# Cosine attention and a dense block on one core: norm steps moved between visits, dense work shifted by one visit, one exponential held back

## The chip, the cores and the metric

The kernel runs on one core of a Trainium2 chip. The core has a matrix engine (TensorE, PE in the profile; its weight loads are PEld), a vector engine (VectorE, DVE), an engine for functions of one element (ScalarE, ACT), a general engine (GpSimd, POOL) and a queue engine (SyncE, SP). They run side by side, each through its own queue in order, and wait for each other through semaphores. The metric is the time of one execution on the device in microseconds (us), as a median over runs.

## The reference

Inputs are q, k and v of shape (8 batches, 12 heads, 448 tokens, 64), a number tau = 0.1, and two weight matrices.

```python
q_n = q / (norm(q, axis=-1) + 1e-6)
k_n = k / (norm(k, axis=-1) + 1e-6)
scores = q_n @ k_n.transpose(0, 1, 3, 2) / tau
attn = exp(scores - max(scores));  attn = attn / (sum(attn) + 1e-9)
x = (attn @ v).transpose(0, 2, 1, 3).reshape(3584, 768)
h = x @ w_in                      # 768 -> 2048
out = maximum(0.01 * h, h) @ w_out    # 2048 -> 768
```

So each batch is attention over normalized queries and keys, and the 3584 rows of all batches then pass a dense block of two layers with a leaky activation.

## The kernel before

**Attention.** The 448 tokens of a batch are taken as 4 blocks of 112 (NT, PK). Heads are handled in 6 pairs (p from 0 to 5), and pairs in 3 groups (g) of four heads. For a pair, `scores` works in two halves. A half is two key blocks: for each one, two matmuls (one head each) write a PSUM tile `sc`, and one exponential on ScalarE (L209) turns it into `pe`. There are two `sc` buffers. When both pairs of a group are done, `sums` multiplies `pe` with ones and `values` multiplies it with v, 16 matmuls each (L216), into the two `pv` buffers. `inverse` takes the reciprocal of the sums on VectorE (L239) and frees its buffer, and `x_write` multiplies and writes x, transposed (L253 and L254 in even batches, L256 in odd ones). `weigh` strings these together, once for each half (s) of the group's values.

**Norms.** They are made one batch ahead. `norm_squares` (L123) squares on VectorE or GpSimd (in the opening on ScalarE too, L121), `norm_reduce` sums 64 elements on VectorE (L126), `norm_root` takes the root as Ln and Exp on ScalarE (L138, L139), `norm_inverse` adds and inverts on VectorE (L143, L144), `norm_apply` scales, mostly on GpSimd in pieces of two heads (L151). `norm_sums` is squares and reduction together. The scaled q and k must then be turned so that the 64 elements lie on partitions: batches 0 to 3 by TensorE (`turn_pair`, L179, with copies on VectorE, L189), later ones by a DMA transpose (`turn`, L168).

**Dense block.** Rows are cut into chunks of 3 or 4 tiles of 128, in turn: chunk c needs x of batch c. `layer1` makes one of 16 groups of 6 matmuls (L274), 384 or 512 columns wide, and the activation on ScalarE (L279); `layer2` makes a group of 16 matmuls (L287), a copy on ScalarE (L293) and the output write on SyncE's queue. Both take their PSUM from two `mm` buffers, which `turn_pair` uses too.

**The order.** It is written out by hand and nothing reorders it. An opening does batch 0. Then a loop runs over batches 1 to 7 and in each over 12 visits (n, a pair and a half). One visit does: the scores of that half; one `weigh` if one is owed (visits 4 and 5, 8 and 9, and 0 and 1 of the next batch); the steps of `after_scores`, where norm steps and loads are set by batch and visit; dense groups, by `fill`; the turns of `after_dense`. `fill` takes groups from a list with a cost each (layer 1 about 1.0 or 1.3, layer 2 2.65) until the running cost reaches a goal. The goal rises evenly with the visits, so that chunk c is worked through from visit 2 of batch c + 1 to visit 1 of batch c + 2; the first chunk has 14 visits.

```python
if b == 1 or (b == 2 and n < 2):
    fill(chunk_end[0] * (12 * (b - 1) + n + 1) / 14)
else:
    c = b - 1 if n >= 2 else b - 2
    start = chunk_end[c - 1]
    fill(start + (chunk_end[c] - start) * ((n - 2) % 12 + 1) / 12)
```

From batch 3 on, the steps for the next batch stand at visits 0 to 7: sums of q at 0, root at 1, sums of k at 2 with the scaling of q, root of k at 3, scaling of k at 4, transposes at 5 and 7. After the loop come the last two `weigh` and what is left of the list.

Of the kernel before, what the change touches and what calls it, by code (L numbers as in the profile page):

```python
# [9 lines left out]
BF16 = mybir.dt.bfloat16  # L10
ACTF = mybir.ActivationFunctionType
# [5 lines left out]
def kernel(  # L17
# [17 lines left out]
    nc = tc.nc  # L35
# [3 lines left out]
    NT = 4  # L39
# [59 lines left out]
    def load_w_out(n):  # L99
        nc.gpsimd.dma_start(  # L100
            out=w_out_sb[:, :, n * NH : (n + 1) * NH], in_=w_out_r[:, :, n * NH : (n + 1) * NH]
        )
# [67 lines left out]
            in_=xn.rearrange("p g t h d -> p (g t h d)"),  # L170
        )

    def turn_pair(b, p):
        g, j = divmod(p, 2)
        tp = pmm.tile([128, 2, NT, PK], BF16, name="mm")
        for i, what in enumerate("qk"):
            xn = st[what + "n", b]
            for t in range(NT):
                nc.tensor.matmul(  # L179
                    out=tp[:, i, t, :],  # L180
                    lhsT=xn[:, g, t, 2 * j : 2 * j + 2, :].rearrange("p h d -> p (h d)"),
                    rhs=ident, is_transpose=True,
                    start=(i == 0 and t == 0), stop=(i == 1 and t == NT - 1),
                )
        for i, what in enumerate("qk"):
            xt = turned(b, what)[:, : NT * HP * PK].rearrange(
                "d (g t j n) -> d g t j n", g=G, t=NT, j=2
            )
            nc.vector.tensor_copy(out=xt[:, g, :, j, :], in_=tp[:, i])  # L189


    def scores(b, p, half):
        qT, kT = st["qT", b], st["kT", b]
        g, j = divmod(p, 2)
        q5 = qT[:, : NT * HP * PK].rearrange("d (g t j n) -> d g t j n", g=G, t=NT, j=2)
        if half == 0:
            st["pe", b, p] = epool.tile([PK, NT, 2, S], BF16, name="pe")
        pe = st["pe", b, p]
        wide = 128 if b > 3 else PK
        for ki in (2 * half, 2 * half + 1):  # L200
            sc = psc.tile([128, 2, 512], F32, name="sc")
            o = ((g * NT + ki) * 2 + j) * PK
            for a in range(2):
                r = slice(64 * a, 64 * a + 64)
                nc.tensor.matmul(  # L205
                    out=sc[:wide, a, :S], lhsT=kT[r, o : o + wide], rhs=q5[r, g, :, j, :],
                    start=True, stop=True,
                )
            nc.scalar.activation(  # L209
                out=pe[:, ki], in_=sc[:PK, :, :S], func=ACTF.Exp, scale=inv_tau  # L210
            )

    def columns(dst, b, g, weights):
        for ki in range(NT):
# [17 lines left out]
    def sums(b, g):  # L232
        sm = ppv.tile([128, S], F32, name="pv")
        columns(sm, b, g, lambda a, ki: ones[:PK, :])
        return sm

    def inverse(b, g, sm):
        st["rs", b, g] = wk.tile([128, S], F32, name="rs")
        nc.vector.reciprocal(st["rs", b, g], sm)  # L239
        if g == 0:  # L240
            x_place(b)

    def values(b, g, s, po=None):
        vb = st["v", b]
        if po is None:
            po = ppv.tile([128, S], F32, name="pv")
        columns(po, b, g, lambda a, ki: vb[:, G * a + g, ki, 32 * s : 32 * s + 32])
        return po

    def x_write(b, g, s, po):  # L250
        rs, x, kt = st["rs", b, g], st["x", b], 2 * g + s
        if b % 2 == 0:
            nc.vector.tensor_mul(x[:, kt, 0:384], po[:, 0:384], rs[:, 0:384])  # L253
            nc.vector.tensor_mul(st["x64", b][:, kt, :], po[:, 384:S], rs[:, 384:S])  # L254
        else:
            nc.vector.tensor_mul(x[:, kt, 64:512], po, rs)  # L256
# [121 lines left out]
    norm_apply(0, "q", V, 2, 3)  # L378
    scores(0, 2, 0)
    sm = sums(0, 0)  # L380
    po = values(0, 0, 0)
    inverse(0, 0, sm)
    scores(0, 2, 1)
    load_w_out(0)
    x_write(0, 0, 0, po)
    scores(0, 3, 0)
    x_write(0, 0, 1, values(0, 0, 1))
    scores(0, 3, 1)
    turn_pair(0, 4)
    turn_pair(0, 5)  # L390
    norm_squares(1, "q", P, 0, 1)
    norm_squares(1, "k", P, 0, 1)
    load(1, "v")
    scores(0, 4, 0)
    sm = sums(0, 1)
    po = values(0, 1, 0)
    inverse(0, 1, sm)
    x_write(0, 1, 0, po)
    scores(0, 4, 1)
    load_w_out(1)  # L400
    norm_reduce(1, "q", 0, 1)
    norm_reduce(1, "k", 0, 1)
    scores(0, 5, 0)
    x_write(0, 1, 1, values(0, 1, 1))
    norm_root(1, "q", 0, 1)
    norm_root(1, "k", 0, 1)
    scores(0, 5, 1)
    norm_inverse(1, "q", 0, 1)
    norm_inverse(1, "k", 0, 1)
    norm_apply(1, "q", P, 0, 1)  # L410
# [18 lines left out]
    def after_scores(b, n):  # L429
        if b + 2 < B and b > 1 and n < 2:  # L430
            load(b + 2, "qk"[n])
        if b + 1 == B:
            return
        if b > 1 and n == 2:
            load(b + 1, "v")
        if b == 1:
            if n == 0:
                load(2, "q")
                norm_sums(1, "q", 1, 2)
                norm_sums(1, "k", 1, 2)  # L440
            elif n == 1:
                load(2, "k")
                norm_root(1, "q", 1, 2)
                norm_root(1, "k", 1, 2)
                norm_sums(1, "q", 2, 3)
                norm_sums(1, "k", 2, 3)
            elif n == 2:
                load(2, "v")
                for what in "qk":
                    norm_inverse(1, what, 1, 2)  # L450
                    norm_apply(1, what, P, 1, 2)
                norm_root(1, "q", 2, 3)
                norm_root(1, "k", 2, 3)
            elif n == 3:
                for what in "qk":
                    norm_inverse(1, what, 2, 3)
                    norm_apply(1, what, P, 2, 3)
            elif n == 5:
                load(3, "q")
            elif n == 6:  # L460
                norm_sums(2, "q")
                load(3, "k")
            elif n == 7:
                norm_root(2, "q")
                norm_sums(2, "k")
            elif n == 8:
                norm_root(2, "k")
                norm_inverse(2, "q")
                norm_inverse(2, "k")
                for g in range(G):  # L470
                    norm_apply(2, "q", P, g, g + 1)
                    norm_apply(2, "k", V if g == 0 else P, g, g + 1)
        elif b == 2:
            if n == 3:
                norm_sums(3, "q")
            elif n == 5:
                norm_root(3, "q")
                norm_sums(3, "k")
            elif n == 6:
                norm_root(3, "k")  # L480
                norm_inverse(3, "q")
                norm_inverse(3, "k")
                for g in range(G):
                    norm_apply(3, "q", P, g, g + 1)
                    norm_apply(3, "k", P, g, g + 1)
        elif n == 0:
            norm_sums(b + 1, "q")
        elif n == 1:
            norm_root(b + 1, "q")
        elif n == 2:  # L490
            norm_sums(b + 1, "k")
            norm_inverse(b + 1, "q")
            norm_apply(b + 1, "q", P)
        elif n == 3:
            norm_root(b + 1, "k")
        elif n == 4:
            norm_inverse(b + 1, "k")
            norm_apply(b + 1, "k", P)
        elif n == 5:
            turn(b + 1, "q")  # L500
        elif n == 7:
            turn(b + 1, "k")

    turns = {
        (1, 3): (1, 2), (1, 4): (1, 3), (1, 5): (1, 4, 5), (1, 10): (2, 0, 1),
        (1, 11): (2, 2, 3), (2, 1): (2, 4, 5), (2, 9): (3, 0, 1), (2, 10): (3, 2, 3),
        (2, 11): (3, 4, 5),
    }

    def after_dense(b, n):  # L510
# [3 lines left out]

    owed = []
    for b in range(1, B):
        for p in range(HP):
            for half in range(2):  # L520
                n = 2 * p + half
                scores(b, p, half)
                if owed:
                    weigh(*owed.pop(0))
                if half == 1 and p % 2 == 1:
                    owed += [(b, p // 2, 0), (b, p // 2, 1)]
                after_scores(b, n)
                if b == 1 or (b == 2 and n < 2):
                    fill(chunk_end[0] * (12 * (b - 1) + n + 1) / 14)
                else:  # L530
                    c = b - 1 if n >= 2 else b - 2
                    start = chunk_end[c - 1]
                    fill(start + (chunk_end[c] - start) * ((n - 2) % 12 + 1) / 12)
                after_dense(b, n)
    fill(spent[0] + 1.0)
    weigh(*owed[0])
    fill(chunk_end[B - 2] - 3.0)
    weigh(*owed[1])
    fill(1e9)

# [34 lines left out]
```

## Time and profile before

| | |
|---|---|
| time, median of 3 runs | 486.72 us (484.1 to 489.21) |
| span of the profiled run | 485.3 us |
| mean granted clock of TensorE | 0.982 of full |
| VectorE, reciprocals of row sums | 24 of 2.96 us |
| VectorE, squares and reduction of a whole q or k | 1.9 and 3.35 us |
| ScalarE, exponentials | 192 of 0.92 us, 0.86 back to back |
| ScalarE, activations of layer 1 | 128 of 0.5 or 0.6 us |
| GpSimd, scaling | 86 pieces of 1.06 us |
| DMA transposes, issue to landing | 5.1 us (q) and 7.3 us (k) in the median, 11.0 at most |

A line of the timeline gives start, length, engine, line of the kernel, what is written from what, shapes and count; in brackets is how long the engine stood idle before it and what it waited for. Matmuls overlap, so the length of a group of them is from its first start to its last end. "PEclk" is the clock that TensorE was granted, as a share of full speed or in tenths.

### The profile page before, as it was taken

What the parts mean: (1) busy time and instruction counts of PE and PEld (TensorE: products, weight loads), DVE (VectorE), ACT (ScalarE), POOL (GpSimd) and SP (SyncE); (2) the same over time, 40 slices, a digit from 0 to 9 for tenths busy, and PEclk for the clock granted to TensorE, in tenths of its full rate; (3) what the DMA queues carried; (4) which work ended last, traced back from release to release, by engine and by line L of the source; (5) the groups of instructions that cost most, each with busy time, mean ns of one, the idle gap of its engine ahead of it and who ended that gap; (6) DMA issues with size and microseconds to landing.
All of it is one profiled execution on the core that took longest, in us unless ns stands there. A gap on an engine that the chain in (4) does not pass through costs nothing.

```text
span 485.3 us, 8021 instructions
## 1 busy us (share of the span) xinstructions
PE 438.5 (90%) x3380; PEld 213.6 (44%) x3392; DVE 217.4 (45%) x265; ACT 265.9 (55%) x429; POOL 127.3 (26%) x152
## 2 busy tenths in 40 slices
PE   0786988899899989998999989997999999989996
PEld 0332454454355544442345434442445444444463
DVE  5967959657632871347412672338403312321000
ACT  3874856546654377455564577454664567433411
POOL 7457160740280047002720036002620000000000
PEclk9999899999999999998999999997999999998999
DMA  9999995194019335924393244215331200120022
GB/s 124 212 197 203 202 148 80 50 135 69 1 29 167 55 53 93 170 64 57 58 148 90 54 70 86 63 49 74 57 58 50 63 20 1 34 65 1 0 66 65
DMA packets 68482, 39.82 MB, mean 82 GB/s; under 512 B 24160, under 2 KB 67680, under 8 KB 68448
## 3 DMA queue, kind: packets, MB, share of 16 engines
q0 software_dynamic: 37728, 22.81, 33.6%
q1 hardware_dynamic: 30720, 16.52, 14.3%
q8 instruction: 26, 0.43, 0.4%
q14 instruction: 8, 0.07, 0.0%
HBM read 45.61 MB, written 11.01 MB: 117 GB/s over the span
## 4 chain that ended last, share of the span: by engine, by line
PE 70%; DVE 14%; ACT 8%; issue 5%; POOL 1%; DMA 1%; DVEq 0%; ACTq 0%; POOLq 0%
PE mm L274 26%; PE mm L287 25%; PE pv L216 10%; PE sc L205 7%; DVE rs L239 5%; ACT pe L209 4%; DVE q_n L123 2%; DVE q_ni L126 2%; ACT hT L279 2%; DVE k_ni L126 2%; PE mm L179 2%; POOL q_n L151 1%; DVE k_n L123 1%; DMA qk_bf<-in_q_dram 1%; ACT osb L293 1%
## 5 line engine op out<-in xcount | busy, mean ns | idle before, releaser
L274 PE MATMUL mm<-xT,w_in_sb 128*128 128x384 bf16 (+1 forms) x756 | 161.9, 362 | 16.2 <-ACT hT L279 5.3
L209 ACT ACTIVATE pe<-sc 112x896 bf16<-112x896 f32 x192 | 165.0, 917 | 15.0 <-PE sc L205 14.9
L287 PE MATMUL mm<-w_out_sb,hT 128*128 128x384 bf16 x896 | 153.3, 326 | 0.1
L239 DVE RECIPROCAL rs<-pv 128x448 f32<-128x448 f32 x24 | 71.0, 2957 | 165.4 <-PE pv L216 165.4
L274 PEld LDWEIGHTS <-w_in_sb 128*128 128x128 bf16 x768 | 72.8, 99 | 102.1 <-issue 45.0
L287 PEld LDWEIGHTS <-hT 128*128 128x128 bf16 x896 | 84.6, 98 | 67.8 <-issue 14.5
L279 ACT ACTIVATE hT<-mm 128x384 bf16<-128x384 f32 (+1 forms) x128 | 68.7, 545 | 68.0 <-PE mm L274 67.3
L293 ACT COPY osb<-mm 128x384 f32<-128x384 f32 x56 | 26.7, 478 | 106.8 <-PE mm L287 81.5
L151 POOL TENSOR_TENSOR q_n<-qk_bf,q_ni 112x512 bf16<-112x512 bf16 x42 | 43.5, 1063 | 92.1 <-DVE q_ni L144 37.0
L205 PE MATMUL sc<-qT,kT 64*112 64x448 bf16 (+1 forms) x384 | 59.6, 379 | 8.8 <-ACT pe L209 5.4
L151 POOL TENSOR_TENSOR k_n<-qk_bf,k_ni 112x512 bf16<-112x512 bf16 x44 | 45.4, 1059 | 16.8 <-DVE k_ni L144 12.4
L216 PE MATMUL pv<-pe,v_bf 112*32 112x448 bf16 x736 | 44.1, 360 | 3.6 <-DVE rs L239 3.6
L91 POOL DMA_DIRECT2D v_bf<-in_v_dram x8 | 7.6, 949 | 110.5 <-PE pv L216 82.9
L205 PEld LDWEIGHTS <-kT 64*112 64x112 bf16 (+1 forms) x384 | 16.4, 113 | 42.6 <-issue 38.0
L216 PEld LDWEIGHTS <-v_bf 112*32 112x32 bf16 x768 | 18.9, 97 | 23.8 <-issue 12.3
L126 DVE TENSOR_REDUCE q_ni<-q_n 112x16 f32<-112x1024 bf16 (+1 forms) x12 | 27.4, 2284 | 0.3
L126 DVE TENSOR_REDUCE k_ni<-k_n 112x16 f32<-112x1024 bf16 (+1 forms) x12 | 27.4, 2284 | 0.3
L216 PE MATMUL pv<-pe,ones 112*32 112x448 bf16 x384 | 23.6, 364 | 0.0
L179 PE MATMUL mm<-ident,q_n 112*128 112x112 bf16 x96 | 9.9, 233 | 12.7 <-DVE q_n L151 11.1
L189 DVE COPY qT<-mm 128x448 bf16<-128x448 bf16 x24 | 9.3, 387 | 25.6 <-PE mm L179 25.3
L256 DVE TENSOR_TENSOR xT<-pv,rs 128x448 bf16<-128x448 f32 x24 | 15.0, 623 | 9.9 <-PE pv L216 8.3
L253 DVE TENSOR_TENSOR xT<-pv,rs 128x384 bf16<-128x384 f32 x22 | 12.2, 556 | 12.7 <-PE pv L216 11.6
(49 smaller groups left out, 150.4 us busy)
## 6 DMA issues: line engine op xcount, KB each, us to landing
v_bf<-in_v_dram POOLq DMA_DIRECT2D x8, 672.0 KB, 8.0
qk_bf<-in_q_dram POOLq DMA_DIRECT2D x6, 672.0 KB, 10.0
qk_bf<-in_k_dram POOLq DMA_DIRECT2D x6, 672.0 KB, 12.6
w_in_sb<-in_moe_w_in_dram POOLq DMA_DIRECT2D x4, 768.0 KB, 18.4
w_out_sb<-in_moe_w_out_dram POOLq DMA_DIRECT2D x2, 1536.0 KB, 19.3
out_dram<-osb SPq DMA_DIRECT2D x16, 168.0 KB, 2.2
out_dram<-osb SPq DMA_DIRECT2D x16, 144.0 KB, 2.0
out_dram<-osb SPq DMA_DIRECT2D x16, 120.0 KB, 1.9
```

The costliest lines, as they stand in the source:

```text
L126: nc.vector.tensor_reduce(st[what + "i", b][:, g0:g1].rearrange("p g a t -> p (g a) t"), squares(b, what, g0, g1).rearrange("p g a t d -> ...
L151: eng.tensor_tensor(out=xn[:, g, :, a : a + step, :].rearrange("p t h d -> p h t d"), in0=x[:, g, a : a + step], in1=ni[:, g, a : a + step ...
L179: nc.tensor.matmul(out=tp[:, i, t, :], lhsT=xn[:, g, t, 2 * j : 2 * j + 2, :].rearrange("p h d -> p (h d)"), rhs=ident, is_transpose=True, ...
L205: nc.tensor.matmul(out=sc[:wide, a, :S], lhsT=kT[r, o : o + wide], rhs=q5[r, g, :, j, :], start=True, stop=True,)
L209: nc.scalar.activation(out=pe[:, ki], in_=sc[:PK, :, :S], func=ACTF.Exp, scale=inv_tau)
L216: nc.tensor.matmul(out=dst[32 * a : 32 * a + 32, :], lhsT=weights(a, ki), rhs=st["pe", b, 2 * g + a // 2][:, ki, a % 2, :], start=(ki == 0 ...
L239: nc.vector.reciprocal(st["rs", b, g], sm)
L256: nc.vector.tensor_mul(x[:, kt, 64:512], po, rs)
L274: nc.tensor.matmul(out=pm[:, :n], lhsT=w_in_sb[:, kt, m * 128 : (m + 1) * 128], rhs=st["x", c][:, kt, :n], start=(kt == 0), stop=(kt == KT ...
L279: nc.scalar.activation(out=st["h", c][:, m, :n], in_=pm[:, :n], func=ACTF.Prelu, alpha=0.01)
L287: nc.tensor.matmul(out=po[:, :NH], lhsT=st["h", c][:, m, j0 : j0 + 128], rhs=w_out_sb[:, m, n * NH : (n + 1) * NH], start=(m == 0), stop=( ...
L293: nc.scalar.copy(out=osb, in_=po[:, :NH])
```

## The change

It alters only the order of work, apart from one item.

- Norm sums and roots from batch 2 on move to visits in which no row sums are due: sums of q and k at visits 2 and 3, roots at 4 and 5, scaling at 5 and 6, transposes at 7 and 9. VectorE is then meant to be free for the reciprocals and the writes of x.
- The goal of `fill` is shifted by one visit (`budget`): the first chunk gets 15 visits, and a chunk's first group comes at visit 2 or 3 of a batch, after the x that it needs has been written.
- In a visit that owes no `weigh` and has a layer 1 group next, the second exponential is issued behind that group's activation (`hold`).
- Batch 3 is turned by DMA, no longer by TensorE (the item that changes instructions), so its key blocks can be loaded 128 columns wide (`wide`).
- In the opening, `inverse` and the second scores of a group stand ahead of `values`, and the norm steps of batch 1 stand earlier.
- At the end, one layer 2 group more stands between the last two `weigh`.

The diff, without its blank lines:

```diff
--- before.py
+++ after.py
@@ -170,9 +170,10 @@
             in_=xn.rearrange("p g t h d -> p (g t h d)"),
         )
-    def turn_pair(b, p):
+    def turn_pair(b, p, tp=None):
         g, j = divmod(p, 2)
-        tp = pmm.tile([128, 2, NT, PK], BF16, name="mm")
+        if tp is None:
+            tp = pmm.tile([128, 2, NT, PK], BF16, name="mm")
         for i, what in enumerate("qk"):
             xn = st[what + "n", b]
             for t in range(NT):
@@ -189,14 +190,15 @@
             nc.vector.tensor_copy(out=xt[:, g, :, j, :], in_=tp[:, i])
-    def scores(b, p, half):
+    def scores(b, p, half, hold=False):
         qT, kT = st["qT", b], st["kT", b]
         g, j = divmod(p, 2)
         q5 = qT[:, : NT * HP * PK].rearrange("d (g t j n) -> d g t j n", g=G, t=NT, j=2)
         if half == 0:
             st["pe", b, p] = epool.tile([PK, NT, 2, S], BF16, name="pe")
         pe = st["pe", b, p]
-        wide = 128 if b > 3 else PK
+        wide = 128 if b > 2 else PK
         for ki in (2 * half, 2 * half + 1):
             sc = psc.tile([128, 2, 512], F32, name="sc")
             o = ((g * NT + ki) * 2 + j) * PK
@@ -206,9 +208,13 @@
                     out=sc[:wide, a, :S], lhsT=kT[r, o : o + wide], rhs=q5[r, g, :, j, :],
                     start=True, stop=True,
                 )
-            nc.scalar.activation(
-                out=pe[:, ki], in_=sc[:PK, :, :S], func=ACTF.Exp, scale=inv_tau
-            )
+            st["exp", ki % 2] = (pe[:, ki], sc)
+            if ki % 2 == 0 or not hold:
+                exponential(ki % 2)
+    def exponential(i):
+        pe, sc = st["exp", i]
+        nc.scalar.activation(out=pe, in_=sc[:PK, :, :S], func=ACTF.Exp, scale=inv_tau)
     def columns(dst, b, g, weights):
         for ki in range(NT):
@@ -378,33 +384,33 @@
     norm_apply(0, "q", V, 2, 3)
     scores(0, 2, 0)
     sm = sums(0, 0)
-    po = values(0, 0, 0)
     inverse(0, 0, sm)
     scores(0, 2, 1)
+    po = values(0, 0, 0)
     load_w_out(0)
+    norm_squares(1, "q", P, 0, 1)
+    norm_squares(1, "k", P, 0, 1)
     x_write(0, 0, 0, po)
     scores(0, 3, 0)
+    scores(0, 3, 1)
     x_write(0, 0, 1, values(0, 0, 1))
-    scores(0, 3, 1)
     turn_pair(0, 4)
     turn_pair(0, 5)
-    norm_squares(1, "q", P, 0, 1)
-    norm_squares(1, "k", P, 0, 1)
     load(1, "v")
     scores(0, 4, 0)
+    norm_reduce(1, "q", 0, 1)
     sm = sums(0, 1)
+    norm_reduce(1, "k", 0, 1)
+    inverse(0, 1, sm)
+    scores(0, 4, 1)
     po = values(0, 1, 0)
-    inverse(0, 1, sm)
     x_write(0, 1, 0, po)
-    scores(0, 4, 1)
     load_w_out(1)
-    norm_reduce(1, "q", 0, 1)
-    norm_reduce(1, "k", 0, 1)
     scores(0, 5, 0)
-    x_write(0, 1, 1, values(0, 1, 1))
     norm_root(1, "q", 0, 1)
     norm_root(1, "k", 0, 1)
     scores(0, 5, 1)
+    x_write(0, 1, 1, values(0, 1, 1))
     norm_inverse(1, "q", 0, 1)
     norm_inverse(1, "k", 0, 1)
     norm_apply(1, "q", P, 0, 1)
@@ -461,50 +467,37 @@
                 norm_sums(2, "q")
                 load(3, "k")
             elif n == 7:
-                norm_root(2, "q")
                 norm_sums(2, "k")
             elif n == 8:
+                norm_root(2, "q")
+                norm_inverse(2, "q")
+                norm_apply(2, "q", P)
+            elif n == 9:
                 norm_root(2, "k")
-                norm_inverse(2, "q")
                 norm_inverse(2, "k")
-                for g in range(G):
-                    norm_apply(2, "q", P, g, g + 1)
-                    norm_apply(2, "k", V if g == 0 else P, g, g + 1)
-        elif b == 2:
-            if n == 3:
-                norm_sums(3, "q")
-            elif n == 5:
-                norm_root(3, "q")
-                norm_sums(3, "k")
-            elif n == 6:
-                norm_root(3, "k")
-                norm_inverse(3, "q")
-                norm_inverse(3, "k")
-                for g in range(G):
-                    norm_apply(3, "q", P, g, g + 1)
-                    norm_apply(3, "k", P, g, g + 1)
-        elif n == 0:
+                norm_apply(2, "k", V, 0, 1)
+                norm_apply(2, "k", P, 1, 3)
+        elif n == 2:
             norm_sums(b + 1, "q")
-        elif n == 1:
+        elif n == 3:
+            norm_sums(b + 1, "k")
+        elif n == 4:
             norm_root(b + 1, "q")
-        elif n == 2:
-            norm_sums(b + 1, "k")
+        elif n == 5:
+            norm_root(b + 1, "k")
             norm_inverse(b + 1, "q")
             norm_apply(b + 1, "q", P)
-        elif n == 3:
-            norm_root(b + 1, "k")
-        elif n == 4:
+        elif n == 6:
             norm_inverse(b + 1, "k")
             norm_apply(b + 1, "k", P)
-        elif n == 5:
+        elif n == 7:
             turn(b + 1, "q")
-        elif n == 7:
+        elif n == 9:
             turn(b + 1, "k")
     turns = {
         (1, 3): (1, 2), (1, 4): (1, 3), (1, 5): (1, 4, 5), (1, 10): (2, 0, 1),
-        (1, 11): (2, 2, 3), (2, 1): (2, 4, 5), (2, 9): (3, 0, 1), (2, 10): (3, 2, 3),
-        (2, 11): (3, 4, 5),
+        (1, 11): (2, 2, 3), (2, 1): (2, 4, 5),
     }
     def after_dense(b, n):
@@ -513,28 +506,34 @@
             turn_pair(to, p)
+    def budget(b, n):
+        at_ = 12 * (b - 1) + n + 1
+        if at_ <= 15:
+            return chunk_end[0] * at_ / 15
+        c, i = divmod(at_ - 3, 12)
+        return chunk_end[c - 1] + (chunk_end[c] - chunk_end[c - 1]) * i / 12
     owed = []
     for b in range(1, B):
         for p in range(HP):
             for half in range(2):
                 n = 2 * p + half
-                scores(b, p, half)
+                hold = not owed and at[0] < len(dense) and dense[at[0]][1] < 2.0
+                scores(b, p, half, hold)
                 if owed:
                     weigh(*owed.pop(0))
                 if half == 1 and p % 2 == 1:
                     owed += [(b, p // 2, 0), (b, p // 2, 1)]
+                if hold:
+                    fill(spent[0] + 0.5)
+                    exponential(1)
                 after_scores(b, n)
-                if b == 1 or (b == 2 and n < 2):
-                    fill(chunk_end[0] * (12 * (b - 1) + n + 1) / 14)
-                else:
-                    c = b - 1 if n >= 2 else b - 2
-                    start = chunk_end[c - 1]
-                    fill(start + (chunk_end[c] - start) * ((n - 2) % 12 + 1) / 12)
+                fill(budget(b, n))
                 after_dense(b, n)
     fill(spent[0] + 1.0)
     weigh(*owed[0])
-    fill(chunk_end[B - 2] - 3.0)
+    fill(chunk_end[B - 2] - 0.1)
     weigh(*owed[1])
     fill(1e9)
```

## The prediction

> **What bounds the kernel now.** I read the busy table, then the slices, then the waits, then the timeline at each long wait.
>
> ```profile
> PE 438.5 (90%) x3380; PEld 213.6 (44%) x3392; DVE 217.4 (45%) x265; ACT 265.9 (55%) x429; POOL 127.3 (26%) x152
> ...
> PE   0786988899899989998999989997999999989996
> ...
> PEclk9999899999999999998999999997999999998999
> ```
>
> TensorE (PE) is busy 90% of the span and every other engine 55% or less, so the end is set by PE's work plus PE's pauses. The granted clock dips in the fifth slice and in three others: 219, 328 and 437 us.
>
> ```profile
> PE sc L205 <- ACT pe L209: 5.4, 11, 1.1
> PE mm L274 <- ACT hT L279: 5.3, 8, 1.3
> PE mm L274 <- DVE xT L253: 4.6, 5, 2.2
> PE mm L274 <- DVE xT L256: 4.5, 2, 2.3
> PE pv L216 <- DVE rs L239: 3.6, 2, 2.3
> ```
>
> Total, times, longest: PE waits for ScalarE (ACT) in many small pieces, for VectorE (DVE) in few long ones. The long ones, PE first, then DVE, where batch 4 begins:
>
> ```profile
> 217.50 0.36 PE L205 MATMUL sc<-qT,kT 64*128 64x448 bf16 x2
> 218.31 0.36 PE L205 MATMUL sc<-qT,kT 64*128 64x448 bf16 x2 [0.44 <-ACT pe L209]
> 218.61 1.25 PE L274 MATMUL mm<-xT,w_in_sb 128*128 128x512 bf16 x4
> 222.13 4.65 PE L274 MATMUL mm<-xT,w_in_sb 128*128 128x512 bf16 x13 [2.27 <-DVE xT L256]
> ```
> ```profile
> 215.73 0.62 DVE L256 TENSOR_TENSOR xT<-pv,rs 128x448 bf16<-128x448 f32 x1
> 216.27 1.89 DVE L123 TENSOR_TENSOR q_n<-qk_bf 112x1024 bf16<-112x1024 bf16 x3
> 218.19 3.35 DVE L126 TENSOR_REDUCE q_ni<-q_n 112x48 f32<-112x3072 bf16 x1
> 221.46 0.62 DVE L256 TENSOR_TENSOR xT<-pv,rs 128x448 bf16<-128x448 f32 x1
> ```
>
> The last write of x (L256, at 221.46) stands in DVE's queue behind 5.2 us of norm sums of the next batch, and the next chunk's first dense group needs it. Then the clock:
>
> ```profile
> 219.00:222.00 3.00, 0.81 (x3) 1.00 0.93 112
> 222.00:226.00 4.00, 3.87 (x11) 0.57 0.66 88
> 332.00:338.00 6.00, 5.68 (x15) 0.50 0.56 76
> 437.00:441.00 4.00, 3.78 (x23) 0.57 0.02 4
> ```
>
> Columns: window, length, PE busy, clock, DMA. After each wait of 2.2 to 2.3 us PE runs near half speed for about 4 to 6 us, so such a wait costs nearly double. Waits of 1.26 and 1.30 us (at 130.66 and 87.04) were not followed by this.
>
> **What the Trainium skill says.** "TensorE: Matmul & The Clock Gate", Part 1: the array runs at half rate after an idle activity window of about 3.4 us that runs freely, and needs a busy one to recover. The trace agrees on half rate (0.50) and on a few us of recovery; here 2.3 us of idling among short bursts sufficed. The same page, on engine queue depths: ACT and DVE are strict FIFO. The trace shows it: the ready x write waits out norm sums it doesn't need. The same page, on weight-path modes: fast weight load needs 128 weights. Weight loads of the score matmuls take 132 ns on average with 112 columns and 94 with 128.
>
> **The change, part by part.** A "visit" is one half pair: 4 score matmuls (0.48 to 0.52 us), perhaps a sum or value product (0.76, 0.87), then dense groups: layer 1 is 1.03 us with 384 columns, 1.35 with 512; layer 2 is 2.7. One exponential is 0.86, one activation 0.5 or 0.6.
>
> *Saved.*
> 1. Batches 4 and 6, visits 0 to 2. Norm sums go to visits 2 and 3, and visits 1 and 2 have dense work again (layer 2 at 1, the first group of the new chunk at 2). The x write of visit 1 then has 2.7 us of layer 2 above it and a free DVE. Batch 4: 0.44 + 2.27 idle; 13 matmuls in 4.6 us where 12 take 2.7 at full clock, so 1.7, and 0.2 in the next group: 4.6. Batch 6: 0.44 + 2.27, then 13 in 5.64 (2.7 lost), 0.2 in the scores: 5.6.
> 2. Batches 3 and 5, same place, three-tile chunks: ACT's Ln waits on the reduction and holds back exponentials and activations behind it. PE pauses 0.52 + 0.28 + 0.87 + 0.49 = 2.2 and 0.58 + 0.28 + 0.87 + 0.52 = 2.25. Roots now follow their sums by two visits: 4.4.
> 3. The end: the last value product waits 2.31 us for the 2.96 us reciprocal that frees its PSUM buffer. One layer 2 group (2.7) now stands between. The slow clock after it costs 0.25 + 0.6 + 0.3 (93 matmuls in 21.3 against 21.0). Together 3.45. The following x write (0.62) lies under five matmuls of the first group (1.1).
> 4. Batch 3 turned by DMA: 48 transposes leave PE. Their three groups take 147.92-146.71, 154.91-153.65, 159.30-158.04: 3.7. Twelve visits of 128-wide weights at 0.04: 0.5. The 12 DVE copies go too, at no gain: PE didn't wait for them.
> 5. Batch 2: the 1.26 at 130.66 (a root on ACT ahead of an activation) and 0.29 beside the turns: 1.55.
>
> Saved: 4.6 + 5.6 + 4.4 + 3.45 + 4.2 + 1.55 = 23.8.
>
> *Paid.*
> 6. The held exponential. Scores have two PSUM buffers. In batches 2, 4, 6, visit 2 has one dense group only. From its start: scores to 0.55, group to 1.9, activation to 2.55, held exponential to 3.45; PE is back at 2.2 and wants that buffer. Queued behind it on PE are the second scores and everything dense. Wait 1.3; three of them 4.0. With two groups PE returns after 3.1 (four tiles) against a loop of 0.4 scores + 1.35 + 0.6 + 0.87 = 3.2, and after 2.6 against 2.9 (three tiles): some 0.2 in each of three visits, 0.6. With three groups nothing. The trace of before has no held exponential; the bounds are 0 (the copy of visit 1 already delays both exponentials) and 2.0 with a slow clock after it, 6 to 9 for three.
> 7. The front. Two reductions of batch 1 now stand on DVE ahead of the second reciprocal. The second needs GpSimd's squares, ready at 37.0 (load-bound at 33.27, unchanged). So the reciprocal starts at 38.3, not 34.45; its end at 41.3 releases the value product, x and the first dense groups (40.97 before, 42.9 after). The third sums start 2.0 later, and so does the third reciprocal. I take 2.0; bounds 0 (if earlier exponentials win it back) and 3.5 (clock).
> 8. Chunk 0, batch 1 visits 0 to 3: ACT holds 8 exponentials, two root groups and the activations. I walked it instruction by instruction: one group fewer done at visit 4 and 0.9 later, evened out by the wait on the reciprocal at visit 9, which DVE sets either way (norm sums start when the last turns are copied). Pay 0.9.
> 9. Batch 2's keys are scaled after all of q on GpSimd (1.03 a piece, six, then two), so the turns of group 1 wait about 0.5; with one empty visit moved next to turns that hide it, 0.7.
> 10. Batch 2: the norm sums of batch 3 (10.5 us on DVE) begin only after the last turn copies, so visit 4's reciprocal is late and the value product of visit 5 waits 0.8. In batches 3 to 6 these sums can start already under visit 1's layer 2, so the reciprocal ends a us before PE asks.
>
> Paid: 4.6 + 2.0 + 0.9 + 0.7 + 0.8 = 9.0.
>
> Nothing: the DMA transposes move from visits 5 and 7 to 7 and 9. k's issue stands behind one output write; about 10.6 us remain until the next batch's scores, against 7.3 (median) and 11.0 (longest) from issue to landing. The output writes that queue behind it have four buffers.
>
> Net 14.8: 486.7 - 14.8 = 471.9.
>
> **The rivals.**
> *A: the held exponential brings the slow clock.* Three waits of 1.3 each followed by 1.9 to 2.9 as in part 1, and the front at 3.5: 472 + 7.2 + 1.5 gives about 481. For: four short bursts between pauses is the pattern at 219. Against: 1.3 us waits so far weren't followed by it.
> *B: the front and the hold cost nothing.* Exponentials run earlier, ACT catches up: 472 - 6 = 466. For: ACT is only 55% busy. Against: the loop in 6 is a chain, not a load.
> *C: keys land late.* If k takes 15 us from issue, batches 4 and 6 wait 4.4 each and batches 3, 5, 7 (13 us of room) 2.0 each, with 2 us of slow clock at all five: 14.8 + 10 = 24.8, so 497, slower than before. For: loads for the batch after start when GpSimd finishes scaling, and they share the DMA engines. Against: the trace before has that overlap already (loads from 243.42, transpose at 243.41) and 11.0 as its longest.
>
> **How the numbers follow.** Main case 0.68 (472), A 0.14 (481, on the edge of 1%), B 0.12 (466), C 0.06 (497, with milder forms near no change). Over 1% is below 481.9: 0.68 + 0.12 and a little more than half of A, some 0.87; within 1% about 0.08; slower 0.05. The range of 464 to 481.5 takes in B, the main case with the bounds of 7 and most of A.
>
> **What would show it.** Right: no PE wait for an x write (L253 or L256 before) over 1 us after the first 60 us; the clock near 1.0 from 210 us to the end; no PE wait for the reciprocal at the end; PE instructions fewer by 48 matmuls; score matmuls waiting about 1.3 us for the exponential three times; the second reciprocal starting near 38 us. Wrong: score matmuls waiting for the DMA transposes, a clock dip after a held exponential, or new waits of PE on DVE at visits 4 and 5, where two batches of norm sums now meet the row sums.

## The result and the profile after

The changed kernel takes 472.82 us (median of 4 runs, 471.53 to 473.38) against 487.59 in the same session: a ratio of 0.9703, 95% interval 0.9644 to 0.9762. The forecast was 472.0, with a range of 464 to 481.5.

From the page of the changed kernel: busy times, PE by slices, granted clock.

```profile
PE 430.0 (91%) x3330; PEld 209.2 (44%) x3344; DVE 214.5 (45%) x253; ACT 266.5 (57%) x429; POOL 127.4 (27%) x152
...
PE   0686689898999999988999999998999999999996
...
PEclk9998899999999999999999999999999999999999
```

PE is busy 8.5 us less (its slow matmuls count in that), and three of the four clock dips are gone: those at 219, 328 and 437 us. The dip in the opening stayed and grew, from one slice to two. The waits of PE in the changed kernel (total, times, longest; L217 is the exponential, L245 the reciprocal, L259 the x write of even batches):

```profile
PE sc L207 <- ACT pe L217: 9.5, 15, 1.2
PE pv L222 <- DVE rs L245: 5.3, 3, 2.9
PE mm L280 <- DVE xT L259: 2.5, 2, 2.2
...
PE sc L207 <- DMA kT<-k_n: 1.8, 1, 1.8
```

No first-layer group waits for an x write of an odd batch any more, and its waits for activations (5.3 us before) have left the list. Waits for exponentials have nearly doubled, from 5.4 us, and one for a transposed k is new. The start of batch 4, PE and then DVE:

```profile
210.00 0.55 PE L207 MATMUL sc<-qT,kT 64*128 64x448 bf16 x4 [1.75 <-DMA kT<-k_n]
...
216.17 2.77 PE L293 MATMUL mm<-w_out_sb,hT 128*128 128x384 bf16 x16
218.88 0.55 PE L207 MATMUL sc<-qT,kT 64*128 64x448 bf16 x4
219.36 1.47 PE L280 MATMUL mm<-xT,w_in_sb 128*128 128x512 bf16 x5
220.76 0.36 PE L207 MATMUL sc<-qT,kT 64*128 64x448 bf16 x2
222.32 0.37 PE L207 MATMUL sc<-qT,kT 64*128 64x448 bf16 x2 [1.20 <-ACT pe L217]
222.62 2.76 PE L280 MATMUL mm<-xT,w_in_sb 128*128 128x512 bf16 x12
```
```profile
216.29 0.62 DVE L262 TENSOR_TENSOR xT<-pv,rs 128x448 bf16<-128x448 f32 x1 [1.13 <-PE pv L222]
216.83 1.89 DVE L123 TENSOR_TENSOR q_n<-qk_bf 112x1024 bf16<-112x1024 bf16 x3
218.75 3.35 DVE L126 TENSOR_REDUCE q_ni<-q_n 112x48 f32<-112x3072 bf16 x1
222.02 1.88 DVE L123 TENSOR_TENSOR k_n<-qk_bf 112x1024 bf16<-112x1024 bf16 x3
```

The x write (L262) now runs as soon as its product is there, and the norm sums come after it. The wait of 2.27 us and the 1.9 us of slow clock are gone; 1.20 us for the held exponential took their place, and the next twelve matmuls run at full speed (2.76 us).

The opening went the other way. DVE, changed kernel:

```profile
36.47 1.22 DVE L126 TENSOR_REDUCE q_ni<-q_n 112x16 f32<-112x1024 bf16 x1 [2.44 <-POOL q_n L123]
38.33 1.22 DVE L126 TENSOR_REDUCE k_ni<-k_n 112x16 f32<-112x1024 bf16 x1 [0.64 <-POOL k_n L123]
39.47 2.95 DVE L245 RECIPROCAL rs<-pv 128x448 f32<-128x448 f32 x1
```

The reciprocal began at 34.45 before and begins at 39.47 now, behind two reductions that wait for GpSimd's squares. The value product that needs its buffer waits, and eight first-layer matmuls after it take 2.67 us at half clock (0.50 from 43 to 46 us):

```profile
42.47 1.37 PE L222 MATMUL pv<-pe,v_bf 112*32 112x448 bf16 x16 [2.89 <-DVE rs L245]
43.77 2.67 PE L280 MATMUL mm<-xT,w_in_sb 128*128 128x384 bf16 x8
```

### The profile page after: what moved, and what is told of

Same layout as the page of the kernel before. It is cut to its first block, busy times and chain, and to the rows that moved or that the text cites. A ratio compares the mean times of both kernels' runs of the same rounds, so it can differ in the third digit from the quotient of the medians.

```text
span 471.6 us, 7915 instructions
## 1 busy us (share of the span) xinstructions
PE 430.0 (91%) x3330; PEld 209.2 (44%) x3344; DVE 214.5 (45%) x253; ACT 266.5 (57%) x429; POOL 127.4 (27%) x152
## 4 chain that ended last, share of the span: by engine, by line
PE 75%; DMA 9%; DVE 7%; ACT 3%; issue 3%; POOL 3%; SPq 0%; POOLq 0%; DVEq 0%; ACTq 0%
PE mm L280 28%; PE mm L293 28%; PE pv L222 11%; PE sc L207 7%; DMA qk_bf<-in_q_dram 5%; DVE rs L245 2%; DMA kT<-k_n 2%; DVE k_ni L126 2%; DMA qk_bf<-in_k_dram 2%; ACT pe L217 2%; ACT hT L285 1%; POOL q_n L151 1%; DVE k_n L123 1%; DVE q_n L123 1%; PE mm L180 1%
## 5 line engine op out<-in xcount | busy, mean ns | idle before, releaser
L217 ACT ACTIVATE pe<-sc 112x896 bf16<-112x896 f32 x192 | 167.4, 917 | 12.2 <-PE sc L207 12.0
L280 PE MATMUL mm<-xT,w_in_sb 128*128 128x384 bf16 (+1 forms) x754 | 154.9, 356 | 3.5 <-DVE xT L259 2.5
L245 DVE RECIPROCAL rs<-pv 128x448 f32<-128x448 f32 x24 | 70.9, 2955 | 146.3 <-PE pv L222 146.3
L280 PEld LDWEIGHTS <-w_in_sb 128*128 128x128 bf16 x768 | 71.7, 99 | 81.9 <-issue 20.9
L207 PE MATMUL sc<-qT,kT 64*128 64x448 bf16 (+1 forms) x384 | 61.6, 380 | 14.3 <-ACT pe L217 9.5
L207 PEld LDWEIGHTS <-kT 64*128 64x128 bf16 (+1 forms) x384 | 16.7, 110 | 52.0 <-issue 45.4
L262 DVE TENSOR_TENSOR xT<-pv,rs 128x448 bf16<-128x448 f32 x24 | 14.9, 622 | 18.1 <-PE pv L222 16.8
L259 DVE TENSOR_TENSOR xT<-pv,rs 128x384 bf16<-128x384 f32 x22 | 12.3, 558 | 22.7 <-PE pv L222 21.6
L180 PE MATMUL mm<-ident,q_n 112*128 112x112 bf16 x72 | 7.4, 233 | 11.8 <-DVE q_n L151 11.2
L123 DVE TENSOR_TENSOR q_n<-qk_bf 112x1024 bf16<-112x1024 bf16 x21 | 14.1, 719 | 4.8 <-DMA qk_bf<-in_q_dram 4.8
```

The source lines that it names most:

```text
L123: eng.tensor_mul(sq, x, x)
L207: nc.tensor.matmul(out=sc[:wide, a, :S], lhsT=kT[r, o : o + wide], rhs=q5[r, g, :, j, :], start=True, stop=True,)
L217: nc.scalar.activation(out=pe, in_=sc[:PK, :, :S], func=ACTF.Exp, scale=inv_tau)
L280: nc.tensor.matmul(out=pm[:, :n], lhsT=w_in_sb[:, kt, m * 128 : (m + 1) * 128], rhs=st["x", c][:, kt, :n], start=(kt == 0), stop=(kt == KT ...
```

## The experiments

Each edit is to the changed kernel. Times are medians, and ratios are to the kernel before in the same session, with their 95% intervals. Since an interval is some 4 us wide and the effects are 1 to 5, each verdict rests on the trace as well. The kernel before took 484.38 to 485.88 us in the three sessions of these runs, so a difference of 1 us between sessions shows nothing. The measure is the changed kernel once more; it ran in one of these sessions only.

> The changed kernel itself, as the measure for the others of this group: 472 to 474 us.

It took 472.91 us, ratio 0.9754 (0.971 to 0.9799), span 470.2.

**The hold taken out.**

```diff
-hold = not owed and at[0] < len(dense) and dense[at[0]][1] < 2.0
+hold = False
```

> The changed kernel with both exponentials issued together everywhere. Theory (the hold only costs): the four waits of 1.06 to 1.20 us in single-group visits and some 0.3 to 0.5 in visits with two groups go, one wait of about 0.3 stays in each single-group visit, so about 3.5 us less, 469. Rival (the hold keeps activations from blocking PE, so it pays elsewhere): waits of the first layer for activations come back as in the kernel before (5.3 us there) and the time is the same or up to 2 us more, 473 to 475.

473.75 us, 0.9766 (0.972 to 0.9812): no gain; the theory as stated fell. PE at the start of batch 4 in this kernel:

```profile
221.07 0.55 PE L207 MATMUL sc<-qT,kT 64*128 64x448 bf16 x4
222.56 0.37 PE L207 MATMUL sc<-qT,kT 64*128 64x448 bf16 x2 [0.94 <-ACT pe L217]
223.37 0.36 PE L207 MATMUL sc<-qT,kT 64*128 64x448 bf16 x2 [0.44 <-ACT pe L217]
```

The hold also brings a dense group into visit 2, whose goal is met already. Without it the visit is empty and the next scores wait 0.94 + 0.44 = 1.38 us, against 1.20. In the first chunk, waits for activations (0.29, 1.02, 0.27) come in place of those for exponentials (1.06, 0.48). So the edit changed two things at once, and the next run separates them.

**The group kept, the exponential not held.**

```diff
-scores(b, p, half, hold)
+scores(b, p, half)
 ...
 if hold:
     fill(spent[0] + 0.5)
-    exponential(1)
```

> The changed kernel with the same dense groups in the same visits, also the one that the hold brings in, but the second exponential issued at once and not behind that group's activation. It tells the order on ScalarE from the place of the group, which taking the hold out as a whole did not. Theory (holding back the exponential itself costs): the waits of 1.2 us in single-group visits fall to 0.3 to 0.4, those in two-group visits go, 2.5 to 3 us less, about 470. Rival (activations then block PE instead): waits of the first layer for activations of about 1 us per visit, no gain, 473.

471.65 us, 0.9738 (0.9703 to 0.9773): about 1 us less, inside the interval, and not the 2.5 to 3 expected. The trace shows where it can be seen. PE at batch 6 in this kernel:

```profile
324.42 1.47 PE L280 MATMUL mm<-xT,w_in_sb 128*128 128x512 bf16 x6
325.82 0.78 PE L207 MATMUL sc<-qT,kT 64*128 64x448 bf16 x4
326.53 2.76 PE L280 MATMUL mm<-xT,w_in_sb 128*128 128x512 bf16 x12
```

The scores go through in one piece. From the last row sums of batch 5 to the first of batch 6 it takes 329.71 - 315.54 = 14.17 us, against 329.59 - 314.19 = 15.40 in the changed kernel: 1.2 us. In batch 4 the wait of 1.20 is gone too, but a wait of 2.19 us for keys brought this profile the slow clock there, and the stretch takes 15.4 us in both. In batches 5 and 7, whose held visits have two or three groups, the same stretches differ by less than 0.3 us. In batches 1 and 2 the waits saved come back as longer waits for the reciprocal of row sums (1.89 and 2.13 us against 1.60 and 0.80), because VectorE's norm sums set that pace. So holding the exponential costs close to what was worked out where a visit has one group: plainly in batch 6, by its wait alone in batch 4, and not in batches 1 and 2. No gain from it shows in this kernel.

**The reductions of the opening put back late.**

```diff
 scores(0, 4, 0)
-norm_reduce(1, "q", 0, 1)
 sm = sums(0, 1)
-norm_reduce(1, "k", 0, 1)
 inverse(0, 1, sm)
 ...
 load_w_out(1)
+norm_reduce(1, "q", 0, 1)
+norm_reduce(1, "k", 0, 1)
 scores(0, 5, 0)
```

> The changed kernel with the two norm reductions of batch 1 put back behind the second group's reciprocal and x write; the rest of the new opening stays. Theory (in the opening the reciprocal waits behind the reduction of squares): the reciprocal starts near 35 us and not at 39.5, the value product's wait of 2.89 us goes, and the scores of batch 1 start at about 50 us and not at 53.9, so 3.5 us less, 469. Rival (the opening is set by loads that land late and by the clock): less than 1 us gained, 472 to 473.

471.07 us, 0.9704 (0.9656 to 0.9753). The reciprocal on DVE:

```profile
34.03 2.96 DVE L245 RECIPROCAL rs<-pv 128x448 f32<-128x448 f32 x1 [0.97 <-PE pv L222]
```

The scores of batch 1 begin at 49.70, against 52.50 and 53.88 in the two profiles of the changed kernel. The wait of 2.89 us is gone: the theory holds, though the time fell by about 2 us and not by 3.5. Part of the gain was lost later, at the keys of batch 4:

```profile
206.25 0.55 PE L207 MATMUL sc<-qT,kT 64*128 64x448 bf16 x4 [2.01 <-DMA kT<-k_n]
206.73 1.44 PE L222 MATMUL pv<-pe,ones 112*32 112x448 bf16 x16
207.94 1.72 PE L222 MATMUL pv<-pe,v_bf 112*32 112x448 bf16 x16
```

Two products that take 0.94 us elsewhere take 1.44 and 1.72 at slow clock. From here to the next row sums (at 223.76) it takes 17.0 us, against 15.4 in the changed kernel, so the slow clock cost 1.6.

**The whole opening as before** (the lines from the second scores to the scaling of batch 1 put back, no diff shown):

> The changed kernel with the whole opening of the kernel before, up to the scaling of batch 1. Theory (the new opening costs 3.9 us, the shift of the first scores of batch 1 between the two traces): 469. Rival (it is the reductions alone that cost, and the earlier second exponentials win something): a little slower than with the reductions put back alone, 469.5 to 470.

469.2 us, 0.9649 (0.9607 to 0.969); scores of batch 1 at 49.76. The two openings without the early reductions are level at that point, so the earlier second exponentials and squares won nothing up to there. The intervals don't tell the two kernels apart.

**The shift of the dense work taken back.**

```diff
-fill(budget(b, n))
+if b == 1 or (b == 2 and n < 2):
+    fill(chunk_end[0] * (12 * (b - 1) + n + 1) / 14)
+else:
+    c = b - 1 if n >= 2 else b - 2
+    start = chunk_end[c - 1]
+    fill(start + (chunk_end[c] - start) * ((n - 2) % 12 + 1) / 12)
```

> The changed kernel with the old goal of dense work (14 visits for the first chunk, chunks from visit 2 to visit 1). Theory (the new places of the norm sums alone end the long waits; the shift adds nothing to that): at the start of batches 4 and 6 only a wait of 0.4 us for an exponential is left, the single-group visits and their held exponentials go, and the time is about 471, 2 us less. Rival (the layer 2 group above the x write is needed): waits of about 1 to 2 us for the x write with the slow clock after them, 3 to 4 us for each of batches 4 and 6, 479 to 481.

471.76 us, 0.9732 (0.969 to 0.9775). PE at the start of batch 4:

```profile
215.94 0.94 PE L222 MATMUL pv<-pe,v_bf 112*32 112x448 bf16 x16
216.95 0.36 PE L207 MATMUL sc<-qT,kT 64*128 64x448 bf16 x2
217.76 0.36 PE L207 MATMUL sc<-qT,kT 64*128 64x448 bf16 x2 [0.44 <-ACT pe L217]
218.06 4.06 PE L280 MATMUL mm<-xT,w_in_sb 128*128 128x512 bf16 x18
```

With nothing dense at visit 1, as before the change, the first group still waits for no x write: 18 matmuls run through. Moving the norm sums is enough there, and the rival falls. What the shift does bring is the spare group at the end, which this kernel lacks: the wait of 2.31 us for the reciprocal is back at 422.32, this time without the slow clock.

**The norm steps of batches 3 to 6 put back, the shift kept** (branch for b > 2 as before: sums at visits 0 and 2, roots at 1 and 3, transposes at 5 and 7):

> The changed kernel with the old places of the norm steps in batches 3 to 6 (sums at visits 0 and 2, roots at 1 and 3, transposes at 5 and 7); the shift of the dense work stays. Theory (norm sums in front of the x write and the root on ScalarE cause the waits; the shift hides only part): the x write ends 4.6 us after its product, of which layer 2 hides 2.7, and exponentials wait for the root at visit 1, so 1 to 2 us in each of the four batches and no clock dip, 477 to 480. Rival (the shift alone carries the gain): 473.

476.43 us, 0.9793 (0.9759 to 0.9828), just under the 477 to 480 expected. PE at the start of batch 4, then two windows (length, PE busy, clock, DMA):

```profile
216.94 1.25 PE L280 MATMUL mm<-xT,w_in_sb 128*128 128x512 bf16 x5
218.51 0.38 PE L280 MATMUL mm<-xT,w_in_sb 128*128 128x512 bf16 x1 [0.32 <-DVE xT L262]
219.86 0.37 PE L207 MATMUL sc<-qT,kT 64*128 64x448 bf16 x2 [0.98 <-ACT pe L217]
221.16 0.56 PE L207 MATMUL sc<-qT,kT 64*128 64x448 bf16 x2 [0.93 <-ACT pe L217]
221.65 3.99 PE L280 MATMUL mm<-xT,w_in_sb 128*128 128x512 bf16 x12
```
```profile
217.35:220.76 3.41, 1.58 (x7) 1.00 1.35 212
220.76:224.17 3.41, 3.02 (x8) 0.50 0.03 9
```

The layer 2 group hides all but 0.32 us of the x write, as expected. The root on ScalarE waits for its reduction and delays the exponentials by 0.98 + 0.93. A clock dip, not expected, follows, though no single wait reaches 1 us: twelve matmuls take 3.99 us, not 2.76. From the last row sums of the batch before to their own first ones, batches 3 to 6 lose 0.9, 2.7, 0.9 and 1.2 us against the changed kernel's second profile, and the wait of 1.7 us for the keys of batch 4 is saved. Each half of the change ends the long x wait alone; the early root is what only the moved norm steps cure.

**Batch 3 turned by TensorE again.**

```diff
-wide = 128 if b > 2 else PK
+wide = 128 if b > 3 else PK
 ...
+(2, 9): (3, 0, 1), (2, 10): (3, 2, 3), (2, 11): (3, 4, 5),
 # and turn(b + 1, ...) only for b > 2
```

> The changed kernel with batch 3 turned by TensorE again, as before, and its score weights 112 wide. Theory (transposes cost PE time one for one, 3.7 us, and 0.5 for the weight width): 477. Rival (they fall into pauses): 473.

475.84 us, 0.9773 (0.9734 to 0.9812). From the second row sums of batch 2 to the last, which includes the turns, 163.14 - 139.16 = 23.98 us against 158.62 - 138.07 = 20.55: 3.4 us, close to the 3.7 worked out. They fell into no pauses. The times alone don't settle it: by medians the run is 2.9 us over the changed kernel, by ratios 0.9.

**The end put back.**

```diff
-fill(chunk_end[B - 2] - 0.1)
+fill(chunk_end[B - 2] - 3.0)
```

> The changed kernel with the last layer 2 group no longer between the last two products with v. Theory (the wait for the reciprocal and the slow clock after it were 3.4 us): the wait of 2.3 us is back at the end, a dip of the clock after it, 476. Rival (the wait alone counts, or the clock doesn't dip here): 475 or less.

477.63 us over five executions, 0.9808 (0.9768 to 0.9849). A sixth took 873.49 us and is the one that was profiled, so the kernel was run once more:

> The changed kernel with the end put back once more, for a profile that can be read. Theory: the wait of 2.3 us for the reciprocal returns at about 421 us, with a dip of the clock after it, 476. Rival: 475 or less, no dip.

476.79 us, 0.9835 (0.9804 to 0.9866). By ratios the two runs stand 2.6 and 3.9 us over the changed kernel. The end on PE, and two windows with the clock:

```profile
420.99 0.93 PE L222 MATMUL pv<-pe,v_bf 112*32 112x448 bf16 x16
424.23 0.94 PE L222 MATMUL pv<-pe,v_bf 112*32 112x448 bf16 x16 [2.31 <-DVE rs L245]
425.10 4.45 PE L293 MATMUL mm<-w_out_sb,hT 128*128 128x384 bf16 x16
```
```profile
421.83:425.24 3.41, 1.10 (x21) 1.00 0.17 50
425.24:428.65 3.41, 3.41 (x12) 0.50 0.00 0
```

The wait is 2.31 us and the layer 2 group after it takes 4.45, not 2.77: 2.3 + 1.7 = 4.0. Here the clock counts nearly as much as the wait.

**Both repairs: reductions late, transposes of k at visit 8.** The first edit as shown, and

```diff
-elif n == 9:
+elif n == 8:
     turn(b + 1, "k")
```

> The changed kernel with the two reductions of the opening put back late and the transposes of k at visit 8, not 9. Theory: the opening gains 3 us as before and the wait of 1.7 to 2.0 us for the keys of batch 4 goes, since the transpose starts about 5 us earlier: 468.5 to 469. Rival (the transpose meets the loads of batch 5 and lands no earlier): 471.

467.68 us, 0.9647 (0.9617 to 0.9677). SyncE's queue in the changed kernel, then in this one:

```profile
199.24 8.21 SPq L168 DMA_TRANSPOSE kT<-k_n  x1
```
```profile
192.06 3.77 SPq L168 DMA_TRANSPOSE kT<-k_n  x1
```

The transpose is issued 7 us earlier by these two profiles, and no score matmul waits for keys. It doesn't land faster: 10.25 us from issue, against 10.71. But it lands at 202.31, and the scores begin at 205.14. The first edit alone gave 471.07, so this one is worth about 3, which fits the wait of 2.0 and the slow clock of 1.6; the two intervals overlap.

**The same without the shift.**

> As the run before it, and with the old goal of dense work. Theory (with the norm sums at their new places the shift is not needed, and without it there are no single-group visits): 1 to 1.5 us less than with the shift, 467 to 468. Rival (the shift pays 1 to 2 us elsewhere): 470.

465.23 us, 0.9598 (0.9568 to 0.9628), the fastest of all: 7.7 us, by medians of different sessions, under the changed kernel. Against the run before it, in the same session, it is 2.45 us faster, and no execution of one overlaps with the other: with the norm sums at their new places the shift costs time. It still has the wait at the end (2.31 us, and the product after it takes 1.60 us, not 0.94). A version that keeps a group for the end as well was not tried.

## Why the prediction was right

The time was met within 1 us, partly because misses cancel. The gain is less sure than the time: 14.8 us in that session and 11.8 in the next, where the kernel before took 484.66 us and not 487.59. The table follows the starts of scores in the two traces. From visit 2 of batch 2 on the changed kernel has one dense group fewer done at each point, so 1.35 us (there) or 2.7 (later) are added to its start. "Lead" is after plus that, less before; "measured" is the change of the lead since the row above; "predicted" sums the items that fall into the stretch. Minus is gain.

| stretch up to | before | after | lead | measured | predicted |
|---|---|---|---|---|---|
| batch 1 | 49.97 | 53.88 | +3.9 | +3.9 | +2.0 |
| batch 2, visit 2 | 108.18 | 112.17 | +5.3 | +1.4 | +1.6 |
| batch 3 | 159.30 | 159.50 | +2.9 | -2.4 | -3.2 |
| batch 4 | 211.19 | 210.00 | +1.5 | -1.4 | -2.5 |
| batch 5 | 269.72 | 265.03 | -2.0 | -3.5 | -3.3 |
| batch 6 | 321.38 | 313.71 | -5.0 | -3.0 | -2.0 |
| batch 7 | 380.97 | 368.74 | -9.5 | -4.5 | -4.3 |
| last 128 matmuls | 460.00 | 445.95 | -14.0 | -4.5 | -3.2 |

In the last row both have the same work left, and nothing is added. The gain of the last row beyond the prediction is in part at the end (item 3), in part in batch 7, where three runs of 18 first-layer matmuls took 3.33, 3.29 and 3.29 us before and take 3.10 now (0.6 us). The numbers below are those of the prediction's items.

1. *Batches 4 and 6:* right in cause and size. Taking back either half of the change alone leaves the x wait at 0.32 us or none, so the prediction, which named both halves together, was right that it goes but did not say that one is enough.
2. *Batches 3 and 5:* right that these pauses go. Of the four, the profile puts the first (0.52 and 0.58) down to an x write on VectorE and not to ScalarE. The early root cost 0.9 us in each of these batches even with the shift in place.
3. *The end:* right in cause. The run that puts it back shows 4.0, not 3.45; the slow clock was sized from that one dip of the kernel before, and it differs from dip to dip. The sizes of items 1 and 3 rest on such dips, so that they came out close is in part luck.
4. *Turns of batch 3:* right, 3.4 us against 3.7 for the transposes.
5. and 10. *Batch 2:* the late reciprocal was put at 0.8 and is 0.80; the held wait was put at 1.3 and is 1.17.
6. *The held exponential:* right as a wait (1.17, 1.20, 1.20 against 1.3), but the account was wrong: the same edit brings in the group without which the visit would be empty and wait 1.38. Only the order on ScalarE is a loss, shown in batch 6 and, by its wait, in batch 4.
7. *The opening:* right in cause, too small in size, and with +3.9 over the bound of 3.5. The squares began at 34.56 and not 33.27, since their load landed later in this profile; and the value product's wait drew the slow clock (2.67 us for eight matmuls). The second profile of the changed kernel, where the squares began at 33.18, shows +2.5, and that is the least of all: in the eight profiles with this opening that can be read, the scores of batch 1 begin between 52.50 and 54.82, which is 2.5 to 4.9 in place of 2.0, in seven of them over the bound. In the three with the reductions late they begin between 48.96 and 49.70.
8. and 9. Right as a sum, +1.4 against 1.6; no run takes the two apart.

*Nothing, for the transposes:* this failed, in the room and not in the landing. Batch 4 waited 1.75 us for its keys in the changed kernel. They landed 10.7 us after their issue at 199.24, within the 11.0 of the trace before. But without the wait the scores would have begun at 208.25, so the room was 9.0 us and not 10.6. The median of 7.3 also stood for two kinds: 11.0 and 9.5 us with loads starting at the same time, 5.0 and 5.0 without. Batch 6 had 8.9 us of room and no wait, since no loads were left by then and its keys landed in 5.1. It is rival C in mild form, for one batch. The run with k at visit 8 shows the cause: a landing as slow, but 13.1 us of room.

Rival A did not come: no dip followed a held exponential in the loop of the changed kernel. Rival B was half right as a possibility, not as a mechanism: about 5 us of the opening and the keys could be had, but by moving two steps, not by ScalarE catching up.

On what the Trainium skill was cited for: "TensorE: Matmul & The Clock Gate", Part 1, speaks of an activity window that runs freely, and the traces show one. Up to 460 us every slow stretch in them lasts 3.41 us or two or three times that, and within a trace the slow stretches start whole multiples of 3.41 us apart (before: at 48.20, 222.28, 331.50 and 437.32). What goes with the slow clock is how little PE was busy in the window of this grid just before it. With the end put back, the wait of 2.31 us lay in one window, PE was busy for 1.10 us of it, and half clock followed. In the run without the shift the same wait fell across two windows, and none followed (window, length, PE busy, clock, DMA):

```profile
417.69:421.10 3.41, 2.33 (x37) 1.00 0.27 81
421.10:424.52 3.42, 2.19 (x23) 1.00 0.00 0
424.52:427.93 3.41, 3.41 (x17) 1.00 0.00 0
```

Between 30 and 460 us of the thirteen traces (the one of 873 us is left out), half clock followed all 23 windows at full clock in which PE was busy for 1.47 us or less, 8 of the 19 with 1.50 to 1.88 us, and none of the 1527 with more. The page asks for an idle window; here one in which PE was 43% busy (1.47 of 3.41 us) was enough. The waits for keys fit this: one of 1.75 us brought no slow clock (1.66 us busy in its window), one of 2.01 did (1.40), and one of 2.61 in the run without the shift did not (it fell across two windows, with 1.96 and 2.25 us busy). The held exponentials of 1.20 us left PE busy for 2.2 us of their windows, which fits that rival A did not come.

## What to carry to other kernels

On an engine that takes its queue in order, work for later belongs behind the writes that another engine is waiting for; ask of every step moved forward what is queued behind it, in the opening as well as in the loop. Count a wait of the matrix engine of 2 us at up to double, since slow matmuls may follow; whether they did here also hung on how the wait fell into the windows of the clock. An experiment that takes an edit out whole can hide that the edit did two things with opposite effects; take them apart before judging.

## What was not expected of the hardware

- The clock can dip without any long wait. With the norm steps put back, waits of 0.32, 0.98 and 0.93 us at the start of batch 4 left PE busy for 1.58 us of one window; the next ran at half clock, and twelve matmuls took 3.99 us. Batch 6 of the same trace has waits of 0.98 and 0.93 us too, but 1.90 us busy, and no dip:

```profile
326.57:329.98 3.41, 1.90 (x10) 1.00 0.67 126
329.98:333.40 3.42, 3.42 (x44) 1.00 0.02 5
```

- How long a DMA transpose of k occupies SyncE's queue depends on when the loads of the batch after were issued: 8.21 us where they had been issued 4.1 us earlier (batch 4 of the changed kernel), 4.83 where it was 7.5 us, 3.2 to 3.3 without loads; and 3.77 where they started together with it (k at visit 8), though that one too took 10.25 us to land. In the changed kernel the output writes behind the transpose of 8.21 us left SyncE's queue only at 207.55, when it was done.
